# A transformer block on one Trainium2 core: the first query tile's score shift taken from the first 512 keys alone, and four key tiles of attention inside the opening

## The chip, the core and the metric

The kernel runs on one core of a Trainium2 chip. The core has a matrix engine (TensorE, PE, with its weight loads shown apart as PEld), a vector engine (VectorE, DVE), an activation engine (ScalarE, ACT), a general engine (GpSimd, POOL) and a queue from which most transfers are issued (SyncE, SP). Each engine runs its own list of instructions and waits for the others by semaphores. Operands lie in SBUF, matmul results in PSUM.

The metric is the device time of one execution in microseconds (us), as the median of the runs made.

## What is computed

A pre-LayerNorm block of two halves over S = 2048 tokens of width D = 576, in float32: attention with 32 query heads of width 18 that share one key and one value head, and a bilinear gated feed-forward half of width 4608.

```python
h  = x + A(layernorm(x))
h2 = h + B(layernorm(h))

def A(x):
    q = (x @ wq).reshape(1, S, 32, 18).transpose(0, 2, 1, 3)
    k, v = x @ wk, x @ wv
    p = softmax(einsum("bhqd,bkd->bhqk", q, k) * 18 ** -0.5)
    return einsum("bhqk,bkd->bhqd", p, v).transpose(0, 2, 1, 3).reshape(1, S, 576) @ wo

def B(x):
    return ((x @ w_gate) * (x @ w_up)) @ w_down
```

A softmax does not change when all scores of a query row are shifted by the same number. The kernel subtracts an upper bound of the scores in place of their true maximum, so that the exponential stays within range; the bound for a query and head is the sum over the head's 18 elements of |q| times the largest |k| of that element over the keys.

## The kernel before

The tokens are cut into 4 blocks of 512 (`NB`, `TB`), a block into 4 tiles of 128 (`NQ`); there are 16 key tiles (`NT`) and 8 groups of 4 heads (`NG`). Float32 products are made of split operands, a high part and the rest, so that a projection of one block (`passes`) is 14 matmul steps.

The order of all instructions is written out by hand (`manual_schedule`): each engine takes its instructions in the order in which the program names them. The functions named `stats`, `apply` and so on below are inner functions of `keys_values` (L140).

**The opening, `keys_values`.** SP loads x, the constants, the key and value weights `wkv` and the first seven heads' query weights `wqr`. For each block b there follow
- `stats` and `scale` (L168, L173): mean and variance of each token on DVE, then the reciprocal root by 18 small instructions on POOL (DVE for block 0);
- `apply` (L181): the normalised rows `xh` on ACT, one instruction a tile; `twice` copies their last 64 columns on POOL or DVE;
- `turn` (L192): transposes on PE, into two PSUM tiles of `ps_s` (tag s, two buffers, which the scores of attention use too) and one of `ps_m` (tag m, one buffer);
- `parts` (L207): the split of the transposed block into `XT` (L93 and L102 on ACT, L94 and L103 on DVE);
- `project` (L218): keys and values of the block in one PSUM tile `psk`;
- `keys` (L229): the high part of the keys with the mean of block 0 taken off (L234, ACT), the largest absolute key element `kabs` (L235, DVE), and in its `rest` the copy `kv` (L239, DVE), the low part (L241, POOL), the rows of `kT` (L242, DVE) and a transfer that doubles them to a second group of partitions (L243, SP).

`queries(0)` is a generator that yields after each step; the opening draws its first tile of seven heads (14 steps at L326, then the split, `tq` = |q| and two stores to `q_dram` by SP). After the keys of all blocks, the opening reduces `kabs` to `kab` (L297), spreads it over 126 partitions with a matmul (`psb`, L299) and makes `G` from it (L301). `bounds` (L357) then multiplies `G` and `tq` to the bound (`psg`, L363), splits it to `m2`, stores it to `m_dram`, and records its maximum in `mx`. `load_m` brings it to the two rows of the query tile `q` that multiply the two fixed rows of `kT`: thus the bound is subtracted inside the score matmul. Last, POOL splits the query weights of the other 25 heads (L308, L309), PE transposes the values (`psv`, L312) and DVE copies them to `V` (L313).

**The loop behind it, in `run`.** A round is two calls of `pair` (L486: scores of two pairs of heads against one key tile at L506, their exponential at L507), between them query steps to the amount of `RATE` = 3.0 (each L335 step counts 1, each tile's end 4), and one `flush` (L514) of an earlier key tile's values (L511) into `acc`. A key tile takes two pairs, a group of four heads 32 pairs, a query block 256. Behind the query steps come rounds without them until seven groups (224 pairs) are done; then `guard` (L387) reads a flag, made from `mx`, on whether a bound was so large (`GUARD`) that exact maxima are needed. `prefetch_q` (L466) loads the next group's queries and bounds from the third key tile on, as soon as `known` says that the bounds of these heads are stored. `down_weights` (L900), one step a round, prepares the feed-forward weights with POOL, DVE and large transfers. The remaining pairs run inside the feed-forward half (`ffn`, L815).

Of the kernel before, what the change touches and what calls it, by code (L numbers as in the profile page):

```python
# [58 lines left out]
class Block:  # L59
# [80 lines left out]
    def keys_values(self):  # L140
# [9 lines left out]
        for b in range(NB):  # L150
            for s in range(NQ):
                sp.dma_start(xs[b][:, s, :], self.x[b * TB + s * P: b * TB + (s + 1) * P, :])
            if b == 0:
                sp.dma_start(self.C, self.cst)
                sp.dma_start(wkv, self.wkv)
                sp.dma_start(wqr, self.wq[:, :, 0:7 * DH])
        w_h = self.pp.tile([P, 5, P], F32R, tag="P", name="w_h")
        w_l = self.pp.tile([P, 5, P], F32R, tag="P", name="w_l")
        pool.memset(self.V, 0.0)
        pool.memset(self.V[:, :, 0:1], 1.0)  # L160
        ksum = p0.tile([P, 1], F32, name="ksum")
# [18 lines left out]

        def apply(b):  # L181
            for s in range(NQ):
                xh = xhs[s] = self.pp.tile([P, 640], F32, tag="P", name=f"xh{b}_{s}")
                r, n = rs[NQ * b + s]
                act.activation(xh[:, 0:D], xs[b][:, s, :], AF.Identity, bias=n, scale=r)

        def twice(eng):

            for s in range(NQ):
                eng.tensor_copy(xhs[s][:, D:], xhs[s][:, 512:D])  # L190
# [25 lines left out]
                    self.split(XT[:, 0:4, sl], XT[:, 4:8, sl], tr)  # L216

        def project(b):  # L218
            psk = psks[b] = (self.ps_f if b % 2 else self.ps_a)(f"psk{b}")
            for i, (w, m) in enumerate(passes(w_h, w_l, self.XT[b])):  # L220
                pe.matmul(psk, w, m, start=(i == 0), stop=(i == 13))

# [6 lines left out]
        def keys(b):  # L229
# [13 lines left out]
                sp.dma_start(f32(self.kT[64:120, sl]), f32(self.kT[0:56, sl]))  # L243
            return rest

        first = self.queries(0)

        act.copy(w_h, wkv)
        pool.tensor_tensor(w_l, wkv, f32(w_h), ALU.subtract)
        w = (slice(None), slice(None), slice(0, 7 * DH))  # L250
        act.copy(self.wq_h[w], wqr)
        pool.tensor_tensor(self.wq_l[w], wqr, f32(self.wq_h[w]), ALU.subtract)
        stats(0, 4)
        scale(0, 4, dve)
        apply(0)
        twice(pool)
        stats(4, 8)
        scale(4, 8, pool)
        turn(0)
        parts()  # L260
        stats(8, 12)
        scale(8, 12, pool)
        project(0)
        apply(1)
        stats(12, 13)
        twice(dve)
        turn(1)
        stats(13, 15)
        for _ in range(14):
            next(first)  # L270
        parts()
        stats(15, 16)
        scale(12, 16, pool)
        mean()
        apply(2)
        twice(dve)
        turn(2)
        next(first)
        q = self.qt[0, 0] = self.qp.tile([P, 2, TB], F32R, tag="q", name="q0_0")
        self.load_q(q, 0, 0)  # L280
        project(1)
        parts()
        late = keys(0)
        apply(3)
        twice(pool)
        late()
        turn(3)
        project(2)
        late = keys(1)
        parts()  # L290
        late()
        wqr = self.otp.tile([P, 5, D - 7 * DH], F32, tag="oT", name="wqr1")
        sp.dma_start(wqr, self.wq[:, :, 7 * DH:])
        rest = keys(2)
        project(3)
        late = keys(3)
        dve.tensor_reduce(kab[0:64], kabs[0:64], AX.X, ALU.max)  # L297
        psb = self.ps_m("psb")
        pe.matmul(psb[:, 0:1], self.C[0:64, C_SEL:C_SEL + P], kab[0:64], start=True, stop=True)  # L299
        dve.tensor_copy(kabq, psb[:, 0:1])  # L300
        dve.tensor_scalar(self.G, self.C[:, C_G:C_G + 64], kabq, None, ALU.mult)  # L301
        self.bounds(0, act.copy, self.pp.tile([H, 2, TB], F32R, tag="P", name="m2_0"))
        self.load_m(q, 0, 0)
        rest()
        late()
        for h0, n in QT[1:]:
            w, o = (slice(None), slice(None), slice(h0 * DH, (h0 + n) * DH)), 7 * DH
            pool.tensor_copy(self.wq_h[w], wqr[:, :, h0 * DH - o:(h0 + n) * DH - o])  # L308
            pool.tensor_tensor(self.wq_l[w], wqr[:, :, h0 * DH - o:(h0 + n) * DH - o], f32(self.wq_h[w]), ALU.subtract)  # L309
        psv = self.ps_a("psv")  # L310
        for t in range(NT):
            pe.transpose(psv[:, t * 32:t * 32 + DH], kv[64:64 + DH, t * P:(t + 1) * P], self.ident[64:64 + DH, 64:64 + DH])  # L312
        dve.tensor_copy(self.V[:, :, 1:1 + DH], psv.rearrange("p (t c) -> p t c", c=32)[:, :, 0:DH])  # L313
        return first


    def queries(self, b):

        pe, act, dve, sp = self.pe, self.act, self.dve, self.sp
        for i, (h0, n) in enumerate(QT):  # L320
            r = n * DH
            psq = self.ps_f(f"psq{b}_{i}")
            w_h, w_l = self.wq_h[:, :, h0 * DH:h0 * DH + r], self.wq_l[:, :, h0 * DH:h0 * DH + r]
            if b == i == 0:
                for k, (w, m) in enumerate(passes(w_h, w_l, self.XT[b])):
                    pe.matmul(psq[:r], w, m, start=(k == 0), stop=(k == 13))  # L326
                    yield 1
                qs = self.qb.tile([P, 2, TB], F32R, tag="qs", name=f"qs{b}_{i}")
                self.split(qs[:r, 0], qs[:r, 1], psq[:r], act.copy)
            else:  # L330

                psr = self.ps_f(f"psr{b}_{i}")
                for k, (w, m) in enumerate(passes(w_h, w_l, self.XT[b])):
                    for o, ps in ((0, psq), (64, psr)):
                        pe.matmul(ps[:r], w[o:o + 64], m[o:o + 64], start=(k == 0), stop=(k == 13))  # L335
                    if k < 13:
                        yield 1
                    if self.tqs and self.tqs[0][0] < max(b, 1) and (k == 12 or k >= 5 and 4 <= self.n_pair % (2 * NT) < 2 * NT - 6):
                        self.bounds(self.tqs[0][0])
                qs = self.qb.tile([P, 2, TB], F32R, tag="qs", name=f"qs{b}_{i}")  # L340
                t = f32(qs[:r, 0])
                dve.tensor_copy(t, psr[:r])
                dve.tensor_tensor(f32(qs[:r, 1]), psq[:r], t, ALU.add)
                dve.tensor_copy(qs[:r, 0], f32(qs[:r, 1]))
                dve.tensor_tensor(qs[:r, 1], f32(qs[:r, 1]), f32(qs[:r, 0]), ALU.subtract)
            tq = self.qb.tile([P, TB], F32R, tag="tq", bufs=5, name=f"tq{b}_{i}")
            dve.scalar_tensor_tensor(tq[:r], f32(qs[:r, 0]), -1.0, f32(qs[:r, 0]), ALU.mult, ALU.max)
            rows = self.q_dram[b, h0 * DH:h0 * DH + r]
            sp.dma_start(rows[:, 0:2, :], f32(qs[:r]))
            sp.dma_start(rows[:, 2, :], f32(qs[:r, 0]))  # L350
            self.tqs.append((b, h0, n, tq))
            yield 0 if b == i == 0 else 4
        if b == NB - 1:
            yield 4
            self.bounds(b)

    def bounds(self, b, copy=None, m2=None):  # L357

        pe, dve, sp = self.pe, self.dve, self.sp
        psg = (self.ps_a if self.in_m else self.ps_m)(f"psg{b}_{self.known[b]}")  # L360
        for i, (_, h0, n, tq) in enumerate(self.tqs):
            r = n * DH
            pe.matmul(psg[:H], self.G[:r, 28 - h0:28 - h0 + H], tq[:r], start=(i == 0), stop=(i == len(self.tqs) - 1))  # L363
        lo, hi = self.known[b], self.tqs[-1][1] + self.tqs[-1][2]
        self.tqs = []
        if m2 is None:
            m2 = self.qb.tile([H, 2, TB], F32R, tag="qs", name=f"m2_{b}_{lo}")
        self.split(m2[:, 0], m2[:, 1], psg[:H], copy or dve.tensor_copy)
        sp.dma_start(self.m_dram[b].rearrange("j h q -> h j q")[lo:hi], f32(m2[lo:hi]))
        dve.tensor_reduce(self.mx[:, self.n_mx:self.n_mx + 1], f32(m2[:, 0]), AX.X, ALU.max)  # L370
        self.n_mx += 1
        self.known[b] = hi

    def flag(self):

# [591 lines left out]
    def run(self):  # L967
# [12 lines left out]
        with ExitStack() as st:  # L980
# [9 lines left out]
            self.mx = cp.tile([H, 8], F32, name="mx")  # L990
            st.enter_context(tc.manual_schedule())
            with tc.tile_pool(name="p0q", bufs=1) as self.p0q:
                self.wq_h = self.p0q.tile([P, 5, D], F32R, name="wq_h")
                self.wq_l = self.p0q.tile([P, 5, D], F32R, name="wq_l")
                self.XT = [self.p0q.tile([P, 9, TB], F32R, tag=f"XT{b}", name=f"XT{b}") for b in range(NB)]
                with tc.tile_pool(name="qb", bufs=2) as self.qb:
                    first = self.keys_values()
# [25 lines left out]
            drain(work)  # L1023
            drain(flag)
            self.steps(lambda: self.n_pair % (2 * NT))
            self.flush(len(self.pend))
            self.pair()
            self.pair()
# [34 lines left out]
                self.ffn(b)  # L1063


RATE = 3.0
P_BUFS = 6

P1, P2, P3, P4, P5, P6, P7 = (0, 0), (1, 1), (6, 2), (2, 6), (3, 3), (4, 4), (5, 5)
# [29 lines left out]
def f32(ap):  # L1099
    return ap.bitcast(F32)  # L1100
# [96 lines left out]
```

## Time and profile before

| | us |
|---|---|
| median of 3 runs (2334.88 to 2343.22) | 2335.07 |
| the profiled execution | 2337.37 |
| its span, from the first to the last instruction | 2335.6 |
| first exponential of attention (L507) starts | 59.57 |
| last query step (L335) starts | 307.4 |
| PE idle, 75.95 to 308.90 | 0.26 |
| PE busy, 50.20 to 58.70 | 2.74 of 8.50 |

How to read it: times of the trace are counted from the span's start. A timeline row gives start, duration, engine, line, operation, the tile written and the tiles read, shapes, the number of merged instructions, and in brackets the idle time before with what ended it. A matmul's duration is modelled and overlaps the next; what one costs in a row of equal ones is the distance of their starts. A group's row gives its count, busy time and mean. The granted clock is a fraction of TensorE's full speed.

### The profile page before, as it was taken

The page shows a single profiled execution, that of the slowest core. Times are in us where ns is not written, and L with a number is a line of the kernel's source. Part 1 is how long each engine was busy: PE and PEld are TensorE (multiplying, and loading weights), DVE is VectorE, ACT ScalarE, POOL GpSimd, SP SyncE. Part 2 cuts the span into 40 slices and gives each one's busy share as a digit, 9 for nine tenths or more (in the row PEclk, how much of TensorE's full clock was granted, in tenths as well). Part 3 has the DMA queues.
Part 4 walks back from the last instruction along what each step waited for, and adds up shares of the span by engine and source line. Part 5 has one row for each costly group of instructions (what it writes and reads, how often), then busy time and mean ns, then how long its engine had stood idle before and what let it go on. Part 6 is the DMA issues. An engine that isn't in the chain of part 4 may idle for free.

```text
span 2335.6 us, 46068 instructions
## 1 busy us (share of the span) xinstructions
PE 2287.6 (98%) x18225; PEld 1601.8 (69%) x18225; DVE 1175.2 (50%) x2064; ACT 1433.0 (61%) x1867; POOL 650.1 (28%) x803
## 2 busy tenths in 40 slices
PE   5999999999999999999999999999999999999999
PEld 4434434676777777767777766767777778888888
DVE  7566644344444445444444445444444476565665
ACT  4788886767676766667676766667676623222322
POOL 3544500122222221222222221312222234333333
PEclk9999999999999999999999999999999999999999
DMA  4588962343334333533433433634333345655453
GB/s 141 192 275 267 311 204 78 94 128 123 118 123 128 123 121 98 183 116 122 127 121 120 123 119 101 186 119 128 123 123 110 115 141 189 197 188 179 168 168 127
DMA packets 157842, 345.16 MB, mean 148 GB/s; under 512 B 16095, under 2 KB 48351, under 8 KB 157623
## 3 DMA queue, kind: packets, MB, share of 16 engines
q1 hardware_dynamic: 155031, 331.56, 44.4%
q0 software_dynamic: 2592, 10.62, 1.5%
q8 instruction: 145, 2.38, 0.4%
q14 instruction: 74, 0.61, 0.1%
HBM read 272.63 MB, written 55.67 MB: 141 GB/s over the span
## 4 chain that ended last, share of the span: by engine, by line
PE 81%; DVE 2%; issue 1%; ACT 1%; DMA 1%; POOL 0%; SPq 0%; DVEq 0%; ACTq 0%; POOLq 0%
PE y L795 17%; PE pg L835 15%; PE acc L511 15%; PE gu L835 12%; PE pu L835 10%; PE s L506 9%; PE yo L634 3%; PE y L753 1%; ACT P L507 1%; PE ye L753 0%; PE tx L683 0%; DMA X<-X 0%; DMA out_dram<-h 0%; DVE h L798 0%; DVE h L635 0%
## 5 line engine op out<-in xcount | busy, mean ns | idle before, releaser
L507 ACT ACTIVATE P<-s 128x1024 f32<-128x1024 f32 x1024 | 1026.3, 1027 | 305.0 <-PE s L506 226.1
L835 PE MATMUL pg<-X,ws 64*128 64x512 f32 x2565 | 699.8, 391 | 0.0
L835 PE MATMUL pu<-X,ws 64*128 64x512 f32 x2565 | 699.8, 391 | 0.0
L803 POOL TENSOR_TENSOR h<-h,tmp 128x288 f32<-128x288 f32 x408 | 318.6, 810 | 878.7 <-ACT tmp L802 877.2
L835 PEld LDWEIGHTS pg<-X,ws 64*128 64x128 f32 x2565 | 477.0, 186 | 59.7 <-DMA wdo<-wd_dram 0.8
L835 PEld LDWEIGHTS pu<-X,ws 64*128 64x128 f32 x2565 | 474.5, 186 | 35.1
L511 PE MATMUL acc<-P,V 128*32 128x512 f32 x4096 | 490.7, 599 | 0.7 <-ACT P L507 0.6
L506 PE MATMUL s<-q,kT 56*128 56x512 f32 x2048 | 437.1, 423 | 5.0 <-ACT P L507 2.3
L795 PEld LDWEIGHTS y<-wdo,room 128*128 128x128 f32 x2856 | 387.7, 189 | 51.9 <-issue 43.3
L795 PE MATMUL y<-wdo,room 128*128 128x288 f32 x2856 | 404.8, 300 | 4.8 <-DVE h L798 4.8
L802 ACT COPY tmp<-y 128x288 f32<-128x288 f32 x408 | 163.0, 400 | 330.4 <-PE y L795 324.8
L798 DVE TENSOR_TENSOR h<-h,y 128x288 f32<-128x288 f32 x544 | 235.7, 453 | 242.8 <-PE y L795 240.1
L506 PEld LDWEIGHTS s<-q,kT 56*128 56x128 f32 x2048 | 194.0, 184 | 208.4 <-ACT P L507 116.3
L835 PE MATMUL gu<-X,ws 64*128 64x512 f32 x2646 | 308.3, 389 | 0.3 <-DMA X<-X 0.2
L93 POOL CAST ws<-wr 128x1152 fp32r<-128x1152 f32 x144 | 168.2, 1168 | 430.9 <-PE pu L835 172.6
L835 PEld LDWEIGHTS gu<-X,ws 64*128 64x128 f32 x2646 | 250.8, 184 | 51.3 <-issue 4.0
L511 PEld LDWEIGHTS acc<-P,V 128*32 128x32 f32 x4096 | 114.4, 109 | 247.7 <-issue 241.9
L94 DVE TENSOR_TENSOR ws<-wr,ws 128x1152 fp32r<-128x1152 f32 x144 | 195.6, 1358 | 79.7 <-POOL ws L93 79.7
L857 DVE TENSOR_TENSOR hf<-pu,g 128x512 f32<-128x512 f32 x95 | 65.7, 692 | 332.2 <-ACT g L853 332.2
L94 DVE TENSOR_TENSOR room<-S,room 128x1024 fp32r<-128x1024 f32 x68 | 83.3, 1225 | 159.0 <-ACT room L93 159.0
L853 ACT COPY g<-gu 128x512 f32<-128x512 f32 x49 | 28.9, 590 | 134.8 <-PE gu L835 134.8
L93 ACT CAST room<-hf 128x256 fp32r<-128x256 f32 (+1 forms) x144 | 73.9, 513 | 49.2 <-DVE hf L857 49.0
(162 smaller groups left out, 1572.0 us busy)
## 6 DMA issues: line engine op xcount, KB each, us to landing
wdo<-wd_dram SPq DMA_DIRECT2D x492, 288.0 KB
wr<-in_wgu_dram SPq DMA_DIRECT2D x144, 576.0 KB
wd_dram<-wd_room SPq DMA_DIRECT2D x20, 1008.0 KB
q<-q_dram SPq DMA_DIRECT2D x64, 216.0 KB
q_dram<-qs SPq DMA_DIRECT2D x16, 504.0 KB
X<-X SPq DMA_DIRECT2D x28, 256.0 KB
wd_dram<-wd_hi SPq DMA_DIRECT2D x7, 1008.0 KB
wd_dram<-wd_src SPq DMA_DIRECT2D x7, 1008.0 KB
```

What stands on the lines that cost most here:

```text
L93: (copy or self.cast)(hi, src)
L94: self.dve.tensor_tensor(lo, src, f32(hi), ALU.subtract)
L506: self.pe.matmul(s_[:, i], self.kT[o:o + 56, t * P:(t + 1) * P], q[o:o + 56, pr], start=True, stop=True)
L507: self.act.activation(p_, s_, AF.Exp, scale=SCALE)
L511: self.pe.matmul(acc[32 * j:32 * j + 32, :], self.V[:, t, :], Ps[j // 2][:, j % 2, :], start=(t == 0), stop=(t == NT - 1), skip_group_chec ...
L634: pe.matmul(y[:, :HD], m, k, start=(i == 0), stop=(i == len(ms) - 1))
L795: pe.matmul(y[:, :HD], m[:, t * P:(t + 1) * P], k, start=(first and j == 0), stop=(j == 2), skip_group_check=True)
L798: dve.tensor_tensor(hs, hs, y[:, :HD], ALU.add)
L802: act.copy(z, y[:, :HD])
L803: pool.tensor_tensor(hs, hs, z, ALU.add)
L835: pe.matmul(ps, w[o:o + 64, wk, c], X[o:o + 64, xk, c], start=(j == 0), stop=(j == 26))
L857: dve.tensor_tensor(hf, pu, g, ALU.mult)
```

## The change

The bounds of the first query tile's seven heads are made from block 0's keys alone, as soon as these exist: `mean`, `keys(0)`, a new function `bound` (the former lines of `psb`, `kabq` and `G`), `queries`' first tile, `bounds` and `load_m` stand between `turn(1)` and the `parts()` of block 1. The flag takes its maximum for these heads from a bound over all keys, made at the end by `highest` without a store.

Eight pairs (the four key tiles of block 0, group 0) are issued in the opening: two before `turn(2)`, two before `turn(3)`, two behind `project(3)` and two behind the last block's keys, with three of the four value flushes. The values are transposed and copied for each block by itself (`turn_values`). The last tiles' statistics move behind block 1's copies; the subtractions of `w_l` and of the first query weights move behind other work of POOL; the 14 steps of the first query tile stand ahead of `turn(1)`. The `xh` tiles and the split `wkv` lie in the space of the query weights, which become separate tiles for each group of heads; the load of the other query weights is issued behind the third block's `kT` transfer, ahead of `project(3)`. `RATE` is 3.1, and an assertion fixes that the rounds end at 224 pairs.

```diff
         act.copy(w_h, wkv)
-        pool.tensor_tensor(w_l, wkv, f32(w_h), ALU.subtract)
-        w = (slice(None), slice(None), slice(0, 7 * DH))
-        act.copy(self.wq_h[w], wqr)
-        pool.tensor_tensor(self.wq_l[w], wqr, f32(self.wq_h[w]), ALU.subtract)
+        act.copy(self.wq[0][0], wqr)
         stats(0, 4)
         scale(0, 4, dve)
         apply(0)
         twice(pool)
+        pool.tensor_tensor(w_l, wkv, f32(w_h), ALU.subtract)
         stats(4, 8)
         scale(4, 8, pool)
+        pool.tensor_tensor(self.wq[0][1], wqr, f32(self.wq[0][0]), ALU.subtract)
         turn(0)
         parts()
-        stats(8, 12)
-        scale(8, 12, pool)
+        stats(8, 10)
         project(0)
         apply(1)
-        stats(12, 13)
         twice(dve)
-        turn(1)
-        stats(13, 15)
         for _ in range(14):
             next(first)
-        parts()
-        stats(15, 16)
-        scale(12, 16, pool)
+        stats(10, 12)
+        scale(8, 12, pool)
+        turn(1)
         mean()
-        apply(2)
-        twice(dve)
-        turn(2)
+        late = keys(0)
+        bound(kabs[0:64, 0:1])
         next(first)
         q = self.qt[0, 0] = self.qp.tile([P, 2, TB], F32R, tag="q", name="q0_0")
         self.load_q(q, 0, 0)
+        tqs = list(self.tqs)
+        self.bounds(0, act.copy, self.pp.tile([H, 2, TB], F32R, tag="P", name="m2_0"))
+        self.load_m(q, 0, 0)
+        late()
+        parts()
+        turn_values(0)
+        stats(12, 14)
         project(1)
+        apply(2)
+        twice(pool)
+        stats(14, 16)
+        scale(12, 16, pool)
+        late = keys(1)
+        self.pair()
+        self.pair()
+        turn(2)
+        late()
         parts()
-        late = keys(0)
+        turn_values(1)
+        project(2)
         apply(3)
         twice(pool)
+        late = keys(2)
+        self.pair()
+        self.pair()
+        self.flush(1)
+        turn(3)
         late()
-        turn(3)
-        project(2)
-        late = keys(1)
         parts()
+        wqr = self.otp.tile([P, 5, D - 7 * DH], F32, tag="oT", name="wqr1")
+        sp.dma_start(wqr, self.wq_in[:, :, 7 * DH:])
+        turn_values(2)
+        project(3)
+        del w_h, w_l
+        late = keys(3)
+        self.pair()
+        self.pair()
+        self.flush(1)
         late()
...
+        turn_values(3)
         dve.tensor_reduce(kab[0:64], kabs[0:64], AX.X, ALU.max)
...
+        self.pair()
+        self.pair()
+        self.flush(1)
+        bound(kab[0:64])
+        self.highest(tqs)
+        for i in range(1, len(QT)):
+            self.query_weights(i)
+            h0, n = QT[i]
+            r = wqr[:, :, (h0 - 7) * DH:(h0 - 7 + n) * DH]
+            self.split_pool(*self.wq[i], r)
         return first
...
+        def bound(to):
+
+            psb = self.ps_f("psb")
+            pe.matmul(psb[:, 0:1], self.C[0:64, C_SEL:C_SEL + P], to, start=True, stop=True)
+            dve.tensor_copy(kabq, psb[:, 0:1])
+            dve.tensor_scalar(self.G, self.C[:, C_G:C_G + 64], kabq, None, ALU.mult)
+
+        def turn_values(b):
+            psv = self.ps_m(f"psv{b}")
+            for t in range(NQ):
+                pe.transpose(psv[:, t * 32:t * 32 + DH], kv[64:64 + DH, (b * NQ + t) * P:(b * NQ + t + 1) * P],
+                             self.ident[64:64 + DH, 64:64 + DH])
+            dve.tensor_copy(self.V[:, b * NQ:(b + 1) * NQ, 1:1 + DH],
+                            psv[:, 0:32 * NQ].rearrange("p (t c) -> p t c", c=32)[:, :, 0:DH])
...
+    def highest(self, tqs):
+
+        psg = self.ps_f("psg_all")
+        self.bound_rows(psg, tqs)
+        self.dve.tensor_reduce(self.mx[:, self.n_mx:self.n_mx + 1], psg[:H], AX.X, ALU.max)
+        self.n_mx += 1
...
-RATE = 3.0
+RATE = 3.1
```

More of the change, by code (lines that the diff above doesn't have):

```diff
@@ L155, in keys_values @@
                 sp.dma_start(wkv, self.wkv)
-                sp.dma_start(wqr, self.wq[:, :, 0:7 * DH])
-        w_h = self.pp.tile([P, 5, P], F32R, tag="P", name="w_h")
-        w_l = self.pp.tile([P, 5, P], F32R, tag="P", name="w_l")
+                sp.dma_start(wqr, self.wq_in[:, :, 0:7 * DH])
+        w_h = self.p0q.tile([P, 5, P], F32R, tag="wq3_0", name="w_h")
+        w_l = self.p0q.tile([P, 5, P], F32R, tag="wq3_1", name="w_l")
+        self.query_weights(0)
         pool.memset(self.V, 0.0)
@@ L182, in apply @@
             for s in range(NQ):
-                xh = xhs[s] = self.pp.tile([P, 640], F32, tag="P", name=f"xh{b}_{s}")
+                xh = xhs[s] = self.p0q.tile([P, 640], F32, tag=f"wq{1 + s // 2}_{s % 2}", name=f"xh{b}_{s}")
                 r, n = rs[NQ * b + s]
@@ L218, in project @@
         def project(b):
-            psk = psks[b] = (self.ps_f if b % 2 else self.ps_a)(f"psk{b}")
+            psk = psks[b] = (self.ps_f if b else self.ps_a)(f"psk{b}")
             for i, (w, m) in enumerate(passes(w_h, w_l, self.XT[b])):
@@ L284, in keys_values @@
+        project(2)
         apply(3)
         twice(pool)
+        late = keys(2)
[3 more added lines that the diff above has]
+        turn(3)
         late()
-        turn(3)
-        project(2)
-        late = keys(1)
         parts()
-        late()
[L292 to L296, printed above, removed]
-        dve.tensor_reduce(kab[0:64], kabs[0:64], AX.X, ALU.max)
@@ L298, in keys_values @@
[L298 to L313, printed above, removed]
-        return first
+        wqr = self.otp.tile([P, 5, D - 7 * DH], F32, tag="oT", name="wqr1")
[3 more added lines that the diff above has]
+        del w_h, w_l
@@ L317, in queries, with query_weights @@
+        return first
+    def query_weights(self, i):
+        self.wq[i] = [self.p0q.tile([P, 5, QT[i][1] * DH], F32R, tag=f"wq{i}_{k}", name=f"wq{i}_{k}") for k in range(2)]
     def queries(self, b):
@@ L322, in queries @@
             psq = self.ps_f(f"psq{b}_{i}")
-            w_h, w_l = self.wq_h[:, :, h0 * DH:h0 * DH + r], self.wq_l[:, :, h0 * DH:h0 * DH + r]
+            w_h, w_l = self.wq[i]
             if b == i == 0:
@@ L359, in bounds @@
         pe, dve, sp = self.pe, self.dve, self.sp
[L360 to L363, printed above, removed]
+        psg = self.ps_f("psg0") if m2 is not None else (self.ps_a if self.in_m else self.ps_m)(f"psg{b}_{self.known[b]}")
+        self.bound_rows(psg, self.tqs)
         lo, hi = self.known[b], self.tqs[-1][1] + self.tqs[-1][2]
@@ L369, in bounds, with bound_rows @@
         sp.dma_start(self.m_dram[b].rearrange("j h q -> h j q")[lo:hi], f32(m2[lo:hi]))
-        dve.tensor_reduce(self.mx[:, self.n_mx:self.n_mx + 1], f32(m2[:, 0]), AX.X, ALU.max)
+        if lo or b:
+            dve.tensor_reduce(self.mx[:, self.n_mx:self.n_mx + 1], f32(m2[:, 0]), AX.X, ALU.max)
+            self.n_mx += 1
+        self.known[b] = hi
+    def bound_rows(self, psg, tqs):
+        for i, (_, h0, n, tq) in enumerate(tqs):
+            r = n * DH
+            self.pe.matmul(psg[:H], self.G[:r, 28 - h0:28 - h0 + H], tq[:r], start=(i == 0), stop=(i == len(tqs) - 1))
+    def highest(self, tqs):
+        psg = self.ps_f("psg_all")
+        self.bound_rows(psg, tqs)
+        self.dve.tensor_reduce(self.mx[:, self.n_mx:self.n_mx + 1], psg[:H], AX.X, ALU.max)
         self.n_mx += 1
-        self.known[b] = hi
     def flag(self):
@@ L992, in run @@
             with tc.tile_pool(name="p0q", bufs=1) as self.p0q:
-                self.wq_h = self.p0q.tile([P, 5, D], F32R, name="wq_h")
-                self.wq_l = self.p0q.tile([P, 5, D], F32R, name="wq_l")
+                self.wq_in, self.wq = self.wq, {}
                 self.XT = [self.p0q.tile([P, 9, TB], F32R, tag=f"XT{b}", name=f"XT{b}") for b in range(NB)]
@@ L1025, in run @@
             self.steps(lambda: self.n_pair % (2 * NT))
+            assert self.n_pair == 2 * NT * (NG - 1)
             self.flush(len(self.pend))
```

## The prediction, as it was made before the result was known

> **What bounds the kernel now.** I read the page first: the span, TensorE's (PE's) share and its 40 slices.
>
> ```profile
> span 2335.6 us, 46068 instructions
> ...
> PE 2287.6 (98%) x18225; PEld 1601.8 (69%) x18225; DVE 1175.2 (50%) x2064; ACT 1433.0 (61%) x1867; POOL 650.1 (28%) x803
> ...
> PE   5999999999999999999999999999999999999999
> ```
>
> PE is the bound everywhere but in the first 58 us. Then I cut the opening and the loop behind it into windows: start:end, length, busy time of PE, PEld, DVE, ACT, POOL, granted clock, DMA share, GB/s.
>
> ```profile
> 50.20:58.70 8.50, 2.74 (x19) 2.25 (x19) 4.46 (x9) 1.26 (x2) 1.15 (x2) 0.72 0.48 155
> 58.70:75.95 17.25, 16.37 (x95) 7.08 (x94) 4.55 (x6) 11.33 (x12) 13.34 (x16) 0.74 0.15 48
> 75.95:308.90 232.95, 232.69 (x1732) 93.13 (x1728) 145.15 (x178) 196.70 (x203) 103.84 (x115) 1.00 0.84 275
> ```
>
> From 75.95 to 308.90 PE idles 0.26 us in 233: whatever work is taken out of this loop is gained in full. ACT has 36 us to spare there. Between 50.2 and 58.7 PE works 2.74 us, and the granted clock is 0.72 on the mean. So there is room ahead of the loop; the question is what filling it delays.
>
> Prices of the loop come from its timeline at full clock (start, duration, line, tile):
>
> ```profile
> 172.84 0.50 PE L506 MATMUL s<-q,kT 56*128 56x512 f32 x2
> ...
> 173.18 0.40 PE L335 MATMUL psq<-XT,wq_l 64*72 64x512 f32 x1
> ...
> 173.89 0.39 PE L506 MATMUL s<-q,kT 56*128 56x512 f32 x2
> ...
> 174.21 1.06 PE L511 MATMUL acc<-P,V 128*32 128x512 f32 x8
> ...
> 175.20 0.50 PE L506 MATMUL s<-q,kT 56*128 56x512 f32 x2
> ```
>
> Start to start, a pair's scores cost 0.33 us, the values of a key tile 0.99, three query steps 0.71 (0.237 each). Two pairs without steps are 1.65 us; the eight moved pairs are worth 4 x 1.65 = 6.6 us here, which is the whole gain on offer in the loop. What before has done by 75.95 is counted by groups over 58.70 to 75.94:
>
> ```profile
> L506 PE MATMUL s<-q,kT 56*128 56x512 f32 x24 | 6.5, 544 | 0.0
> L511 PE MATMUL acc<-P,V 128*32 128x512 f32 x40 | 6.2, 696 | 0.0
> L335 PE MATMUL psr<-XT,wq_h 64*126 64x512 f32 x10 | 4.5, 525 | 0.0
> ...
> L335 PE MATMUL psr<-XT,wq_l 64*126 64x512 f32 x5 | 2.6, 516 | 0.0
> ```
>
> That is 12 pairs, 5 key tiles of values and 15 steps: at loop prices 3.96 + 4.95 + 3.56 = 12.5 us of work in 17.25.
>
> **The change, part by part.** Rows of the opening that carry the steps (PE, ACT, DVE, POOL):
>
> ```profile
> 23.40 2.64 PE L199 MATMUL tr<-C,xh 128*128 128x128 f32 x16
> ...
> 26.62 0.71 PE L326 MATMUL psq<-XT,wq_h 128*126 128x512 f32 x2
> ...
> 63.47 0.63 PE L335 MATMUL psq<-XT,wq_h 64*126 64x512 f32 x1
> ...
> 63.89 0.63 PE L335 MATMUL psq<-XT,wq_l 64*126 64x512 f32 x1
> ...
> 22.18 3.14 ACT L185 ACTIVATE xh<-x,n,ya 128x576 f32<-128x576 f32 x4 [2.74 <-POOL n L177]
> ...
> 25.23 1.90 ACT L93 CAST XT<-tr 128x1024 fp32r<-128x1024 f32 x2
> ...
> 35.77 0.69 ACT L234 ACTIVATE kk<-psk,nmean 64x512 fp32r<-64x512 f32 x1
> ...
> 59.57 1.03 ACT L507 ACTIVATE P<-s 128x1024 f32<-128x1024 f32 x1 [5.68 <-PE s L506]
> ...
> L108 DVE BATCH_NORM_STATS2 bsa<-x 128x6 f32<-128x288 f32 x8 | 3.1, 430 | 0.0
> ...
> 28.40 2.36 DVE L94 TENSOR_TENSOR XT<-tr,XT 128x1024 fp32r<-128x1024 f32 x2
> ...
> 30.79 0.69 DVE L103 TENSOR_TENSOR XT<-trt,XT 64x512 fp32r<-64x512 f32 x1
> ...
> 46.91 0.69 DVE L239 COPY kvw<-psk 128x512 f32<-128x512 f32 x1
> ...
> 8.96 1.53 POOL L249 TENSOR_TENSOR w_l<-kvw,w_h 128x640 fp32r<-128x640 f32 x1 [7.52 <-ACT w_h L248]
> ...
> 16.52 0.24 POOL L190 COPY xh<-xh 128x64 f32<-128x64 f32 x1 [0.52 <-ACT xh L185]
> ...
> 17.12 0.24 POOL L118 TENSOR_SCALAR va<-mv 128x4 f32<-128x4 f32 x1 [0.36 <-DVE mv L109]
> ...
> 21.92 0.23 POOL L177 TENSOR_SCALAR n<-n 128x4 f32<-128x4 f32 x1
> ...
> 41.62 0.77 POOL L241 TENSOR_SCALAR kk<-kvw,C,nmb 64x512 f32<-64x512 f32 x1
> ```
>
> Prices: a block's transposes 3.2 us (23.40 to 26.62), a projection 14 x 0.237 = 3.3 (at half clock 0.43 a step, 63.47 to 63.89), the scale of a block on POOL 5.0 (17.12 to 22.15, 18 instructions), apply 3.1, statistics some 0.96 a tile of 128 tokens (a quarter of L108's 3.1 and of four short aggregates), the casts and subtractions of XT 3.1 on DVE, an exponential 1.03. Each engine takes its instructions in the order written; L241's row shows it, whose inputs stood by 36.5 us (L234's row) and which ran at 41.62 behind four copies. So I walk the new order with these prices, handing over at 0.05 us.
>
> *To the first pair.* Up to project(0) nothing moves on PE. On POOL w_l now goes ahead of scale(4, 8), behind the copies that end at 16.76: the scale runs 18.3 to 23.4, and apply(1) starts at 23.4 (before 22.2). wq_l, moved behind it, is there at 24.9, which holds the third query step; the 14 steps end at 27.8. DVE waits for apply(1) with twice, then stats(10, 12) end at 28.7, so nmean is at 29.1, keys 0 at 29.9, kabs at 30.6. turn(1) ends at 31.1; psb and G follow to 31.95, the query split and tq to 33.2, psg, its cast and its subtraction to 34.9. The queue of the transfers (SP) is walked by its rows:
>
> ```profile
> 33.61 0.69 DVE L94 TENSOR_TENSOR qs<-psq,qs 126x512 fp32r<-126x512 f32 x1 [0.27 <-ACT qs L93]
> ...
> 34.77 0.90 SPq L350 DMA_DIRECT2D q_dram<-qs  x1
> ...
> 38.96 0.67 SPq L430 DMA_DIRECT2D q<-q_dram  x2
> ...
> 54.64 0.28 SPq L369 DMA_DIRECT2D m_dram<-m  x1
> ...
> 56.38 0.53 SPq L436 DMA_DIRECT2D q<-m_dram  x2
> ...
> 58.71 0.79 PE L506 MATMUL s<-q,kT 56*128 56x512 f32 x2
> ```
>
> L94's end (34.30) to the load of q is 4.7 us, so that load goes out at 37.3; the store of m waits behind it (37.9), its load goes out at 39.7 and lands within 1.8 (56.91 to 58.71): 42.0. The copy of kT, moved behind both, goes out at 40.2 (0.8 to issue) and lands near 42.8 with the same 1.8; what hides it is that PE is later still, and it costs nothing up to 44.6: DVE reaches kT(0) at 35.6 and only then the subtractions of block 1, to 38.7; psv(0) needs their buffer, project(1) starts at 39.2 and ends at 44.6. PE has idled 31.5 to 38.7, and I charge project(1) half clock until 43.8: 2.3 us.
>
> *Two block cycles.* After a projection ends: scores 0.7, keys and two exponentials on ACT (first free buffer after 1.75), transposes to 5.0 (they share the two score buffers), the last cast and subtraction to 7.25, psv 0.6, projection 3.3: 11.1 us. Block 2 adds 1.3, because kT(1) on DVE waits for L241's kind on POOL behind scale(12, 16) (43.4 to 48.4), with the subtractions of XT queued behind it; and 1.6 for half clock after PE's idle 49.6 to 53.1. project(2) ends near 58.5, project(3) at 69.6. Values of key tile 0 and 1 (0.99 each) lie inside ACT's waits.
>
> *To the loop.* Pairs 5, 6, values, kv copy (L239's kind) and psv(3) run to 72.3, pairs 7, 8 and values to 73.95, psb, G and psg_all to 75.3, DVE's reduction frees psr's buffer at 75.7. New psb and psg_all cost 0.8 on PE here; psv and V in four parts cost 0.2 to 0.44 on DVE each (its smallest row to the undivided copy), inside the cycle. POOL's splits of wq start at 72.5 and their first two parts end by 74.7: 1 us of cover. The load of wqr goes out at 62, 10 us ahead of its reader.
>
> **Sum.** The loop starts at 75.7 with 8 pairs and 3 key tiles done, 2.64 + 2.97 = 5.6 us of the 12.5. Behind by 12.5 - 5.6 = 6.9, ahead by 75.95 - 75.7 = 0.25: +6.6 us. Then one wait is new. The bounds of group 1 come in round 8 in both (3.0 or 3.1 steps a round), but that is pair 23 now and pair 15 before.
>
> ```profile
> 79.21 0.43 PE L363 MATMUL psg<-tq,G 126*32 126x512 f32 x1
> ...
> 85.36 4.28 SPq L436 DMA_DIRECT2D q<-m_dram  x2
> ```
>
> From psg to the end of that last issue are 10.4 us, with 1.8 to land 12.2, behind the stores of wd on the same queue; from psg to pair 33 there now are 1.6 + 4 x 1.65 + 10 x 0.237 = 10.6. Stall: 1.6 us, bounds 0 and 4.3 (another issue as long as L436's). In all +8.2 us.
>
> The profiled execution took 2337.37 us, 1.8 beyond its span; so 2345.6 in such a one, and from the median 2335.07: 2343.3. Bounds: never idle more than before would start the loop at 58.7 + 0 (delta -10.4); half clock all along gives +21 (below). The forecast case spans 2338 to 2349.
>
> The half clock is the softest term: 3.9 us for two gaps. The Trainium skill, page "TensorE: Matmul & The Clock Gate", section "What's actually happening", says that the gate halves the clock after an idle window of about 3.4 us and opens after a busy one as long, in windows that run free. Windows above agree as far as they go: 0.72 mean where PE was mostly idle. By that rule each gap would cost 1.5 to 3.1 us, 3.0 to 6.1 in all, and the time would be an estimate of 2342.4 to 2345.5.
>
> **Rivals.**
>
> *The clock stays at half from 38.7 until the loop.* It decides if PE's short bursts between waits never fill a stretch well enough. For it: 58.70 to 75.95, where PE was busy 16.4 of 17.25 and still got 0.74. Against it: a projection and the pairs' scores behind it are 4 to 6 us without a gap, three times over. Price at 0.43 for 0.237, 0.81 more: 21 further slow steps 4.1, the transposes behind the second exponential 2 x 1.3, scores 1.1 (half of them beside ACT), values 3 x 0.8, and the loop's first 3.4 to 7 us at half, 2.5: 12.7. Time 2356.
>
> *The order written is not the order run*, so that pairs fill gaps and hold up nothing. It decides where the loop starts before 67.5. Place: kT(1) and the subtractions behind it, and the transposes behind the exponentials. Price: start at 58.7 + 5.6 = 64.3, delta 64.3 - 69.1 = -4.8 without the stall. Time 2330: not slower. Against it L241's row.
>
> *The pairs are free* and the loop starts as early as 58.7: 2324.7. The serial chain of cycles speaks against it.
>
> **Chances.** Forecast 0.65, half clock 0.22, order 0.10, free 0.03. This kernel's measurement tells 0.5% from no change, 11.7 us: under 2323.4 or over 2346.7. Slower is the half clock and 0.08 of the forecast's upper end: 0.30; faster 0.03; within 0.67. The range 2333 to 2353 leaves out some 0.08 below and 0.12 above.
>
> **What would show it.** The first exponential near 45 instead of 59.6; transposes of blocks 2 and 3 waiting for ACT P; DVE kT waiting for POOL about 3 us at block 1; the third projection ending near 70; the first two-part query step near 75.7; PE idle about 1.6 us at pair 33; the loop 4 rounds shorter. A loop start before 70 or after 81 would make the prediction wrong, as would a loop whose work does not shrink by 6.6 us.

## The result and the profile after

The changed kernel takes 2350.9 us (median, 2350.43 to 2352.98), before in the same comparison 2337.34; the ratio is 1.0056 [1.0034, 1.0078]. The forecast was 2343.3 in a range of 2333 to 2353: the side and the range were right; the change costs 13.6 us between the two medians and 8.2 were forecast, so the size was some 5 us short. The profiled execution took 2350.61 us, before 2337.37: 13.2 us to explain.

The page of the changed kernel, its first lines:

```profile
span 2348.8 us, 46073 instructions
...
PE 2289.4 (97%) x18228; PEld 1608.2 (68%) x18228; DVE 1165.5 (50%) x2065; ACT 1433.2 (61%) x1867; POOL 648.3 (28%) x807
```

PE is busy for the same time within 2 us (2289.4 to before's 2287.6); most of the 13 us is idle time of PE. The opening on PE's timeline (idle time before, and what ended it, in brackets):

```profile
36.28 0.58 PE L257 MATMUL psv<-C,kvw 18*128 18x18 f32 x4 [5.98 <-DVE XT L103]
...
42.09 0.73 PE L549 MATMUL s<-q,kT 56*128 56x512 f32 x4
43.89 2.00 PE L200 MATMUL tr<-C,xh 128*128 128x128 f32 x16 [1.07 <-ACT P L550]
...
50.65 0.42 PE L257 MATMUL psv<-C,kvw 18*128 18x18 f32 x4 [4.32 <-DVE XT L103]
...
56.02 0.73 PE L549 MATMUL s<-q,kT 56*128 56x512 f32 x4
...
63.08 0.42 PE L257 MATMUL psv<-C,kvw 18*128 18x18 f32 x4 [2.87 <-DVE XT L103]
...
68.41 0.74 PE L549 MATMUL s<-q,kT 56*128 56x512 f32 x4
...
74.53 0.50 PE L549 MATMUL s<-q,kT 56*128 56x512 f32 x2
```

The first pair comes at 42.1 (forecast 44.6), the loop starts at 74.53 (75.7). Three waits for XT, 13.2 us in all, stand ahead of the values and the projections. What the loop had done by 80.08 is counted by groups from 74.5 on:

```profile
L367 PE MATMUL psq<-XT,wq 64*126 64x512 f32 x7 | 2.2, 407 | 0.0
L554 PE MATMUL acc<-P,V 128*32 128x512 f32 x16 | 2.1, 605 | 0.0
L367 PE MATMUL psr<-XT,wq 64*126 64x512 f32 x7 | 2.0, 405 | 0.1
L549 PE MATMUL s<-q,kT 56*128 56x512 f32 x8 | 2.0, 446 | 0.0
```

With the opening's 8 pairs and 3 key tiles that is 12 pairs, 5 key tiles and 7 steps at 80.08. Before had 12, 5 and 15 at 75.95, so 8 steps more, 1.9 us at the loop's price: the changed kernel would have done as much at 82.0, and is 82.0 - 75.95 = 6.0 us behind. The forecast for the opening was 6.6. But at the flag's transpose, where both have the same 224 pairs done, it is 14.25 us behind (the changed kernel, then before):

```profile
334.40 0.18 PE L424 MATMUL psx<-C,mx 32*1 32x32 f32 x1
```

```profile
320.15 0.18 PE L381 MATMUL psx<-C,mx 32*1 32x32 f32 x1
```

8.2 us more are lost inside the loop, where before had lost next to nothing behind 75.95; 1.0 us comes back by the end. Of the 8.2, 5.1 are idle time of PE (5.4 from 80.08 to its last round of query steps, to before's 0.3) and 3.1 are a longer busy time for the same matmuls. The loop's waits of PE, by who ended them (total, times, longest), from 75 to 320 us:

```profile
PE psq L367 <- DVE qs L374: 3.1, 2, 2.7
PE s L549 <- DMA q<-m_dram: 1.5, 1, 1.5
PE psr L367 <- DVE qs L375: 0.7, 3, 0.3
```

The 1.5 us are group 1's bounds, forecast at 1.6. The 3.8 us on DVE's copies of a finished query tile are new. The longest of them can be followed back over four engines (the timelines of POOL, DVE and PE, then two windows: length, busy time and count of PE, PEld, DVE, ACT and POOL, granted clock, DMA share, GB/s):

```profile
164.85 0.57 POOL L967 DMA_DIRECT2D wd_src<-in_wd_dram  x1 [11.67 <-DMA wd_dram<-wd_src]
174.14 3.20 POOL L973 TENSOR_TENSOR wd_src<-wd_src 128x288 f32<-128x288 f32 x4 [8.71 <-DMA wd_src<-in_wd_dram]
177.28 1.99 POOL L981 CAST wd_hi<-wd_src 128x864 fp32r<-128x864 f32 x2
```

```profile
178.22 3.24 DVE L987 TENSOR_TENSOR wd_src<-wd_src,wd_hi 128x864 f32<-128x864 f32 x2 [7.80 <-POOL wd_hi L981]
181.38 0.68 DVE L374 COPY qs<-psr 126x512 f32<-126x512 f32 x1
```

```profile
182.11 0.45 PE L367 MATMUL psq<-XT,wq 64*72 64x512 f32 x1 [2.71 <-DVE qs L374]
```

```profile
185.00:186.00 1.00, 1.00 (x6) 0.47 (x4) 0.17 (x1) 0.51 (x1) 1.00 (x2) 0.50 0.87 283
186.00:187.00 1.00, 1.00 (x6) 0.33 (x3) 0.00 (x0) 0.52 (x1) 1.00 (x2) 0.50 0.56 201
```

A feed-forward weight piece is loaded into a place whose store has to land first; POOL's sums wait for the load, DVE's subtraction (L987) for POOL, and the copy of the query tile (L374) stands behind the subtraction in DVE's queue although its data were ready. PE's next query tile waits for the PSUM place, and behind the idle come some 3.4 us at half clock (0.51 on the mean from 184.3 to 187.7). At that clock they cost some 1.7 us of the 3.1; where the other 1.4 went was not traced.

### The profile page after: what moved, and what is told of

Its sections match the earlier page's. It is cut to its first block, busy times and chain, and to the rows that moved or that the text cites. A ratio compares the mean times of both kernels' runs of the same rounds, so it can differ in the third digit from the quotient of the medians.

```text
span 2348.8 us, 46073 instructions
## 1 busy us (share of the span) xinstructions
PE 2289.4 (97%) x18228; PEld 1608.2 (68%) x18228; DVE 1165.5 (50%) x2065; ACT 1433.2 (61%) x1867; POOL 648.3 (28%) x807
## 4 chain that ended last, share of the span: by engine, by line
PE 81%; DVE 1%; issue 1%; ACT 1%; POOL 1%; DMA 0%; SPq 0%; DVEq 0%; ACTq 0%; POOLq 0%
PE y L838 17%; PE acc L554 15%; PE pg L878 15%; PE gu L878 12%; PE pu L878 10%; PE s L549 9%; PE yo L677 3%; PE y L796 1%; ACT P L550 1%; POOL h L846 0%; PE ye L796 0%; PE tx L726 0%; DMA X<-X 0%; DMA wdo<-wd_dram 0%; POOL ws L93 0%
## 5 line engine op out<-in xcount | busy, mean ns | idle before, releaser
L878 PEld LDWEIGHTS gu<-X,ws 64*128 64x128 f32 x2646 | 256.9, 184 | 44.9 <-issue 4.1
L93 ACT CAST room<-hf 128x256 fp32r<-128x256 f32 (+1 forms) x144 | 73.9, 513 | 49.1 <-DVE hf L900 48.8
```

What stands on the lines that cost most here:

```text
L93: (copy or self.cast)(hi, src)
L878: pe.matmul(ps, w[o:o + 64, wk, c], X[o:o + 64, xk, c], start=(j == 0), stop=(j == 26))
```

## The experiments

A ratio stands against before on the same chip; "loop start" is the first pair behind the opening, "tile waits" are the loop's waits of PE on the two query copies, both from the profiled execution.

| kernel | median us | ratio | loop start | tile waits us |
|---|---|---|---|---|
| the changed kernel | 2350.9 | 1.0056 [1.0034, 1.0078] | 74.5 | 3.8 |
| after_again, the same | 2353.6 | 1.0069 [1.0056, 1.0082] | 77.1 | 4.1 |
| a_low_later | 2348.0 | 1.0045 [1.0029, 1.0062] | 73.9 | 0.2 |
| a_low_again, the same | 2351.1 | 1.0061 [1.0047, 1.0075] | 73.7 | 0.6 |
| b_rate | 2346.0 | 1.0030 [1.0019, 1.0041] | 59.0 | 2.5 |
| b_low_later | 2337.9 | 1.0008 [0.9996, 1.0020] | 58.9 | 0.5 |
| a_no_pairs | 2354.3 | 1.0071 [1.0054, 1.0088] | 78.0 | 0.2 |
| a_warm | 2347.7 | 1.0046 [1.0029, 1.0063] | 71.6 | 3.8 |
| a_parts_first | 2352.1 | 1.0065 [1.0045, 1.0086] | 68.2 | 3.8 |
| a_three | 2338.5 | 1.0011 [1.0000, 1.0021] | 68.9 | 0.5 |
| b_warm | 2336.5 | 1.0001 [0.9990, 1.0012] | 58.3 | 1.6 |
| early_bound | 2339.5 | 1.0014 [1.0004, 1.0024] | 49.6 | 1.9 |
| early_bound2 | 2337.2 | 1.0003 [0.9994, 1.0012] | 51.1 | 0 |

**Where the loop loses.** Theory: the query tiles' ends fall, at 3.1 steps a round, against the weight pieces in a phase in which DVE holds up PE. Rivals: the transfers pace the loop as a whole, or one execution's chance. The first edit moves the two subtractions and the store of each piece one round later, in the changed kernel and in before; the second gives before the new rate.

```diff
-            for d, f in ((6, lambda p=p: store(p)), ...
-                         (2, ... high(p)), (4, ... low(p, 0)), (5, ... low(p, 1))):
+            for d, f in ((7, lambda p=p: store(p)), ...
+                         (2, ... high(p)), (5, ... low(p, 0)), (6, ... low(p, 1))):
```

```diff
-RATE = 3.0
+RATE = 3.1
```

*a_low_later*

> The changed kernel, with the two subtractions and the store of each feed-forward weight piece one round later. Theory (DVE's subtraction of a weight piece waits for POOL, POOL for a transfer, and the copy of the query tile stands behind it in DVE's queue, so PE waits at the change of query tiles): PE's waits on DVE's query copies fall from 3.8 us to under 1, the half clock behind the longest of them goes, time about 5 us under the changed kernel (2346). Rival (the loop is paced by its transfers as a whole): the waits appear at other places and the time stays within 1 us of the changed kernel's.

*b_rate*

> The kernel before with a rate of 3.1 alone: four rounds fewer with query steps, four more without (ACT bounds those, 0.4 us each). Theory (the change of query tiles falls against the weight pieces in another phase at 3.1, and this phase makes PE wait for DVE): waits of PE on DVE's query copies of 2 us or more appear, time 3 to 8 us over before. Rival (the waits come from the loop's shorter start, not from the rate): no such waits, time 1 to 2 us over before.

*b_low_later*

> The kernel before with the two subtractions and the store of each feed-forward weight piece one round later: the control to the same edit in the changed kernel. Theory (before has no such waits to lose): within 1.5 us of before. Rival (the edit helps wherever it stands): 2 to 4 us under before.

*after_again*

> The changed kernel as it is, once more, on one chip with the next. Theory (the waits at the change of query tiles belong to the rate of 3.1 and come in every execution): its trace again shows a wait of PE on DVE's query copies of 2 us or more and a wait for group 1's bounds; 1.004 to 1.007 of before. Rival (they were chance of one execution): waits under 1 us in all.

*a_low_again*

> The changed kernel with the weight pieces' subtractions and store one round later, once more. Theory: no such waits again, 3 to 6 us under the changed kernel of the same chip. Rival: within 1.5 us of it.

The waits of PE in the loop, in the second trace of the changed kernel, then with the later pieces, then of before at 3.1:

```profile
PE psq L367 <- DVE qs L374: 3.7, 2, 2.8
PE s L549 <- DMA q<-m_dram: 1.9, 1, 1.9
PE psr L367 <- DVE qs L375: 0.4, 2, 0.2
```

```profile
PE psr L367 <- DVE qs L375: 0.4, 2, 0.2
PE psq L367 <- DVE qs L374: 0.2, 1, 0.2
```

```profile
PE psq L335 <- DVE qs L342: 1.8, 1, 1.8
PE s L506 <- ACT P L507: 0.8, 2, 0.4
PE psr L335 <- DVE qs L343: 0.7, 3, 0.3
```

The waits come again in the second trace, ahead of the same tiles (the long one ends at 187.3 there, in a trace that starts its loop 2.6 us later), and go with the edit; the wait for group 1's bounds goes with them, since the pieces' stores stand behind these small transfers now. They are no chance. At 3.1 before shows such waits too, and its time grows by more than the 1.6 us of its four rounds without steps (0.3% are 7 us). In its trace the rounds with query steps end at 306.1, to before's 308.0: four rounds, 6.6 us by the prediction's price, are gone from them, and 1.9 are seen. The new opening at 3.0 (a_no_pairs below) has tile waits of 0.2. So the rate is at the root. But it is not alone: kernels at 3.0 show tile waits of 1.6 and 1.9 us in two traces (b_warm, early_bound), so the phase is near the edge there as well. The gain in time is smaller than was expected: 2.5 us between the medians on the same chip, 2.9 on the first pair of comparisons, with intervals that overlap, against 3 to 6; it lies between the theory and the rival. The control came out 2.3 us over before (1.0008), where less than 1.5 either way was expected, with an interval that includes no change: the edit does not help wherever it stands. So the traces settle where the waits come from; what they cost in time is less sure, and why the medians gain less than the traces is open.

**What the opening's length is.** Theory at first: the exponentials ahead of the transposes. a_no_pairs takes the eight calls of `pair` and the three of `flush` out of the opening, at 3.0.

> The changed kernel's opening without its eight pairs and its value flushes, with a rate of 3.0, so that all pairs lie in the loop again (same work in all). Theory (most of the opening's length is the new order, the pairs add 9 us to it by the exponentials ahead of the transposes): loop start near 65.5, time some 3 us over the kernel before. Rival (the pairs are the cost, the new order is free): loop start at 60 or earlier, time no longer than before.

It was a miss on both sides: without the pairs the loop starts later. DVE around block 2, and PE ahead of blocks 2 and 3, in this kernel:

```profile
43.86 0.67 DVE L240 COPY kvw<-psk 128x512 f32<-128x512 f32 x1
47.46 0.74 DVE L243 SCALAR_TENSOR_TENSOR kT<-kk,C 64x512 fp32r<-64x512 f32 x1 [2.93 <-POOL kk L242]
48.13 2.34 DVE L94 TENSOR_TENSOR XT<-tr,XT 128x1024 fp32r<-128x1024 f32 x2
```

```profile
51.25 0.61 PE L257 MATMUL psv<-C,kvw 18*128 18x18 f32 x4 [6.61 <-DVE XT L103]
...
64.80 0.61 PE L257 MATMUL psv<-C,kvw 18*128 18x18 f32 x4 [4.54 <-DVE XT L103]
```

The transposes stood by 44.6, yet the subtractions that make XT began at 48.13: the key rows (kabs, the copy kv, the wait for POOL, kT) are ahead of them in DVE's queue. This chain sets a block's cycle here. In the changed kernel, with the pairs, it does so in block 2 (kT starts at 46.86 behind a wait of 2.62 for POOL); in block 3 kT had ended at 59.77, and the subtractions began behind the cast of the transposes, which follows the exponentials:

```profile
59.95 2.36 DVE L94 TENSOR_TENSOR XT<-tr,XT 128x1024 fp32r<-128x1024 f32 x2 [0.17 <-ACT XT L93]
```

So the two chains end within 0.2 us of each other there, and the pairs lie inside the cycle: from a projection's end to the next values are 8.56 and 7.06 us with them, 8.96 and 6.89 without. They cost next to nothing, and with them PE is busier and the clock higher (0.67 on the mean from 50 to 80 us without them, 0.89 with them).

a_parts_first puts the subtractions ahead of the key rows and the values behind the next projection; a_warm fills PE's gaps.

```diff
         turn(2)
-        late()
         parts()
-        turn_values(1)
         project(2)
+        late()
+        turn_values(1)
```

```diff
+        def warm(n):
+            e = self.ps_f("warm")
+            for i in range(n):
+                pe.matmul(e, w_h[:, 0], self.XT[0][:, 0], start=(i == 0), stop=(i == n - 1))
...
+        warm(24)
         parts()
         turn_values(0)
```

*a_parts_first*

> The changed kernel with the split of blocks 1 to 3 ahead of the last steps of the keys of the block before, and the turn of the values behind the next projection. Theory (what sets a block's cycle is DVE's queue: the key rows that wait for POOL stand ahead of the subtractions; the pairs hide in the gaps): projections of blocks 2 and 3 start 2 to 3.5 us earlier each, until the exponentials ahead of the transposes end last; loop start 68 to 71, time 3 to 6 us under the changed kernel (2345 to 2348). Rival (the exponentials already end last): loop start within 1 us of 74.5, no gain.

*a_warm*

> The changed kernel with 24, 16 and 10 matmuls of no use (128x512, into a PSUM tile that nobody reads) in PE's three gaps ahead of the values of blocks 0, 1 and 2. Theory (half clock costs 2.3 us in the second block's projection, 1.6 in the third's and 1.8 in the fourth's): projections take 3.3 us each, the loop starts 4 to 5.5 us earlier, time 4 to 5 under the changed kernel. Rival (the gaps themselves cost, the clock does not): the projections are shorter but other waits end last, less than 1.5 us gained.

Both move the loop's start: a_parts_first to 68.2, as expected, a_warm to 71.6 (its projections take 3.4 us each; 4 to 5.5 earlier was expected and 2.9 came). In time a_warm is lower than the changed kernel by 0.1 of a percent with overlapping intervals, a_parts_first not at all: behind its start PE waits 2.7 us for POOL's split of the query weights, which itself stood 4.0 us for their load; PE's clock is down behind that, and the tile waits of 3.1 + 0.7 us stand as before.

```profile
PE psq L367 <- DVE qs L374: 3.1, 2, 2.6
PE psq L367 <- POOL wq L97: 1.8, 1, 1.8
PE psq L367 <- POOL wq L98: 0.9, 1, 0.9
```

**All of it together.** a_three has the order of a_parts_first, 10 and 16 matmuls of no use around block 1's projection, the later pieces, the load of the other query weights right behind `apply(3)` and their first split ahead of the last key rows.

> Three mendings of the changed kernel at once: the split of each block ahead of the key rows, matmuls of no use in the gaps around block 1's projection, the weight pieces one round later; and the query weights' first split ahead of the last key rows. Theory (opening 6 us, loop 8 us): loop start near 67, no waits on DVE in the loop, time 8 to 12 us under the changed kernel, about that of before (2336 to 2341). Rival (the loop's length is set by the transfers from its start to its end whatever PE does): an earlier start is given back, time within 4 us of the changed kernel.

It is at 1.0011 of before, as the theory says, and 15 us under the changed kernel on the same chip, more than the 8 to 12 expected and more than the single mendings add up to in time. The wait for POOL's split that followed the start of a_parts_first is gone in it. Its flag's transpose stands at 322.0, 12.4 us ahead of the changed kernel's and 1.9 behind before's. So what was mended in opening and loop together is the whole loss. The parts were not measured apart beyond what the table shows.

**A version to beat both.** early_bound keeps the old order of the opening and makes the first tile's bounds from block 0 where DVE idles; early_bound2 also splits the first other query weights earlier and spreads what is left over the loop's first rounds. b_warm fills before's gaps from 50 to 58 us.

```diff
         late = keys(0)
+        bound(kabs[0:64, 0:1])
+        self.bounds(0, dve.tensor_copy, ...)
+        self.load_m(q, 0, 0)
         apply(3)
...
+                        next(self.after_first, None)
```

*early_bound*

> The old order of the opening, all pairs in the loop, a rate of 3.0, but the first query tile's bounds from block 0 alone, made while DVE idles at 39 to 42 us; the loop starts behind the last projection, and the values of blocks 1 to 3 and the bound over all keys follow the loop's first round. Theory (the early bound is good, the changed kernel's order of the opening is what costs): loop start at 51 to 53 instead of 58.7, time 6 to 10 us under before (2328 to 2332). Rival (the weights of the feed-forward half or the splits of the query weights pace the loop's first 250 us): the start comes earlier, but PE's waits grow in the loop, and less than 3 us are left.

*early_bound2*

> The old order of the opening with the early bound, all pairs in the loop, rate 3.0; the first split of the query weights goes ahead of the last key rows, and the values of blocks 1 to 3, the bound over all keys and its maximum follow one a round from the loop's second round on. Theory (PE can go from the last projection straight into the loop): first query step of the loop at 50 to 53 instead of 59.8, time 5 to 9 us under before. Rival (the transfers pace the loop): the start comes as said, and PE waits more later; less than 3 us are left.

*b_warm*

> The kernel before with 6, 10 and 3 matmuls of no use in PE's gaps between 50 and 58.7 us, to hold the clock up. Theory: the first six rounds of the loop run at full clock and lose 1 to 2 us instead of 4.8; time 3 to 4 us under before (2334). Rival (the loop's start waits for POOL's weight splits anyway, which end at 67): 1 us or less gained.

None beats before. The early bound works: the first pair comes at 49.6 and 51.1. But each start meets the next thing that is late. In early_bound PE waits 5.8 us behind its first pair for POOL's split of the query weights. PE's waits in early_bound2 from 50 to 320 us, the longest four:

```profile
PE psg_all L406 <- DVE G L252: 3.9, 1, 3.9
PE psq L365 <- DVE kvw L240: 1.9, 1, 1.9
PE psr L365 <- DVE kvw L240: 1.5, 1, 1.5
PE psg L406 <- DVE os L563: 0.5, 1, 0.5
```

These 7.8 us are as much as the start is earlier (58.7 to 51.1). They stand at the left-over steps (the values' copies, the bound over all keys); whether an early bound without them would win was not tried. b_warm's rival was right: its start waits 1.6 us for POOL's splits, and nothing is gained.

## Why the prediction held, and where it fell short

- The opening's term was right in size, in part by luck: 6.0 us behind instead of 6.6, loop start at 74.5 instead of 75.7, with two errors that cancel. "Up to project(0) nothing moves on PE" was wrong: w_l, moved off POOL's start, let DVE's scale of block 0 finish 2.6 us earlier (last section), and the first pair came 2.5 us early. Against that stands a term that the sum left out: half clock was charged for two gaps, and the third and last projection, behind a third gap, took 5.0 us instead of 3.3. Without the early scale the loop would have started at some 77 (an estimate, 74.5 + 2.6).
- The two block cycles otherwise came as priced: 13.9 us from the first pair at 42.1 to 56.0 (forecast 13.9), then 12.4 to 68.4 (11.1; the slow projection makes up the difference). Their links stand closer together than the prediction has them. The queue of the key rows was named for block 2 alone, at 1.3 us; in block 3 it ends 0.2 us ahead of the exponentials' chain. So the exponentials, priced as a link of the cycle, can be taken out without a gain, as a_no_pairs shows.
- The stall at group 1, 1.6 us, was measured at 1.5 and 1.9.
- The half clock in the opening was charged at 3.9 us. The three projections took 5.3, 5.0 and 5.0 us, to 3.4 each in a_warm, 5.1 in all; a_warm starts the loop 2.9 us earlier, since other waits then end last.
- The step that failed: "whatever work is taken out of this loop is gained in full". It was read from a loop at 3.0 in which PE idled 0.26 us. The change alters the rate, and the prediction costed the rate only as rounds that fall away. In the changed kernel's loop PE idles 5.5 us up to its last query step, where the prediction has 1.6, and runs 3.4 us at half clock. The matmuls of eight pairs did leave the loop, and their 6.6 us did not come off its time. In the sum's own terms: opening 6.0 (forecast 6.6), stall 1.5 (1.6), 6.7 that no term holds, 1.0 back by the end: 13.2.

```profile
74.53:322.20 247.67, 242.18 (x1775) 98.13 (x1774) 140.32 (x181) 200.81 (x205) 111.38 (x127) 0.99 0.79 255
```

- The row of before held a warning: with a DMA share of 0.84 the transfers leave little room in that loop, and the prediction looked at PE and ACT alone there. That they pace the loop as a whole is not shown: with the pieces' steps one round later the waits go, and none comes up elsewhere.
- Of the rivals, the half clock did not hold through the opening (0.89 on the mean from 50 to 80), and the order written was the order run: the waits above are those of queues in order. The pairs were nearly free, as the last rival has it, but the loop did not start at 58.7 for that: the new order of the opening costs the time.
- That the time lies in the range is luck in part. 2350.9 is 7.6 us from the forecast and 5.1 from the half-clock rival's 2356, which did not occur; the prediction gave 0.67 to a time between 2323.4 and 2346.7.

## What to carry to other kernels

A loop without idle time on its bounding engine shows that nothing is late at this phase, not that nothing is close: look at the engine whose queue is shared by the loop's own steps and by work with transfers behind it, and look at the transfers' share, before counting removed work as gained. When a step is moved forward, list what it is moved ahead of in every engine's queue: here the key rows that nobody needed yet held up the subtractions that everybody waited for. Work that fills a gap can be free, as the pairs here, while the order made for it is not.

## What was not expected of the hardware

DVE's smallest instructions with two inputs took eight to nine times as long beside POOL's. In before, two of block 0's scale (128x4) stood at 1.52 and 1.35 us, others of this size at 0.16; just then POOL ran its subtractions of 1.53 and 1.43 us (L249's row in the prediction starts at 8.96). DVE in before:

```profile
8.80 0.16 DVE L125 TENSOR_TENSOR ta<-ta,va 128x4 f32<-128x4 f32 x1
8.99 1.52 DVE L130 SCALAR_TENSOR_TENSOR ya<-ta,yia 128x4 f32<-128x4 f32 x1
10.55 1.35 DVE L124 TENSOR_TENSOR ta<-ya 128x4 f32<-128x4 f32 x1
```

In the changed kernel POOL has nothing to subtract there, and the same two take 0.16:

```profile
8.96 0.16 DVE L130 SCALAR_TENSOR_TENSOR ya<-ta,yia 128x4 f32<-128x4 f32 x1
9.15 0.16 DVE L124 TENSOR_TENSOR ta<-ya 128x4 f32<-128x4 f32 x1
```

The transposes of block 0 start 2.6 us earlier for it (the changed kernel, then before):

```profile
11.66 3.67 PE L200 MATMUL tr<-C,xh 128*128 128x128 f32 x16 [11.66 <-ACT xh L186]
```

```profile
14.23 3.67 PE L199 MATMUL tr<-C,xh 128*128 128x128 f32 x16 [14.23 <-ACT xh L185]
```

The Trainium skill, page "SBUF — State Buffer", states in its section on the two separate sides of SBUF ("🔬 SBUF: two separate sides") that VectorE and GpSimd share a pair of ports, that a VectorE instruction with two SBUF inputs contends for it, and that the one that comes second is blocked for the whole of the other's instruction; both slow instructions have two SBUF inputs, and their times agree with that.

The clock went to half inside the busy loop as well: behind a wait of only 2.7 us for some 3.4 us, and in the second trace, where the wait was 2.75, for some 7 (186.6 to 193.5).
